# A fused linear-attention and GEGLU kernel: the head halves of batch 0 loaded in the order of use, and its first units in another order

## Chip, cores and metric

One core of one Trainium2 chip. The metric is the device time of one execution in microseconds (us); a quoted time is the median of several executions, in brackets lowest and highest. All executions that are compared were fast, with a granted TensorE clock of 0.99 to 1.00. Ratios are the mean time of one kernel's fast runs over that of the other's in the same rounds, so not quite the ratio of the medians.

## The reference

```python
q_p = concat(relu(q) * cos, relu(q) * sin)      # by position, batch 8, heads 8, seq 576, dim 64
k_p = concat(relu(k) * cos, relu(k) * sin)
kv  = k_p^T v ;  z = sum_s k_p                  # per head, 128 x 64 and 128
x   = (q_p kv) / (q_p z + 1e-6)                 # heads side by side: 4608 x 512
out = (gelu(x @ w_gate) * (x @ w_val)) @ w_out  # 512 -> 1536 -> 512
```

## The kernel before

Everything is scheduled by hand; each engine runs its instructions in the order of the program. A *front* brings batch 0 to its first 128 columns of transposed x. *Units* follow: a gate (four matmuls, then Gelu on ACT) and a value (four matmuls, then a product on VectorE), for one of twelve slices `jt` of 128 hidden channels and some columns of x (`*A` is columns 0 to 255, `*Bw` 256 to 575). While the first units run, the remaining tiles of batch 0 are still normalized and transposed between them. "Dummies" are matmuls on junk, meant to keep the TensorE clock up. An *evacuation* copies a result of TensorE out of the tile `ps`, whose last-but-one index is called a bank; a *hole* is time in which TensorE has nothing to do between two groups of matmuls. `sk` and `sq` scale k and q by cosine or sine, a *numerator* is q_p kv, a *norm* the division by q_p z. "Guards" are copies of one element into a weight tile: the weight loads, issued by GpSimd, must wait for them.

```python
load(kf, k, 0, 0, 4, nc.scalar)      # heads 0-3; the other half of its rows on the SP queue
load(kf, k, 0, 4, 8)
# ... memsets, iota
load(qf, q, 0, j1=2)                 # tiles 0 and 1 of q
load(vf, v, 0, 0, 4)
load(vf, v, 0, 4, 8)
load(qf, q, 0, j0=2)
# ... tables, identity
dummies(26)
for h0 in (0, 4):
    for j in range(NJ + 1):
        sk(j, 0, "v", h0, h0 + 4)                        # k scale with cosine: VectorE
        sk(j, 1, "v" if j < 2 else "s", h0, h0 + 4)      # with sine: VectorE or ACT
nc.scalar.copy(wg_sb[0:2, 0, 0:1], qf[0:2, 7, 1, D - 1:D])   # guard: weights after q has landed
load_w(0, 2); load_w(2, 4); load_w(4, 8)
for j in range(2):
    sq(j, 0, "v"), sq(j, 1, "s")
    q_by_pe(0, j, j, None)                               # transposes
dummies(3)
q_evac(0, 0, 0, "v")
cast_v(0, 0, 2, "v"); cast_v(0, 2, 4, "s")
kv_half(0, 0, 4, None)                                   # k^T v of heads 0-3
q_evac(0, 1, 1, "v")
dummies(2)
cast_v(0, 4, 6, "v"); cast_v(0, 6, 8, "s")
kv_evac(0, 0, 4, "v")
kv_half(0, 1, 5, "s")                                    # heads 4-7
# ... numerators of tiles 0 and 1, norms on VectorE, transposes of x tile 0, of q tile 2
gate(0, 0, 0, 128, 5); gate(0, 1, 0, 128, 4)
# ... units, with X(t) = transposes of x tile t and Y(t) = its numerators and norm between them
```

Of the kernel before, what the change touches and what calls it, by code (L numbers as in the profile page):

```python
# [10 lines left out]
BF16 = mybir.dt.bfloat16  # L11
# [5 lines left out]
def kernel(  # L17
# [10 lines left out]
    nc = tc.nc  # L28

    B, H, S, D = q.shape  # L30
# [4 lines left out]
    CT = C // 128  # L35
# [40 lines left out]
    def load(dst, t, b, h0=0, h1=H, even=None, odd=None, j0=0, j1=NJ + 1):  # L76
        runs = t[b, h0:h1].rearrange("h (i r) d -> i h r d", r=9)
        for s, r0, n, eng in ((1, 5, 4, odd), (0, 0, 5, even)):
            n = min(n, j1)
            (eng or nc.sync).dma_start(  # L80
                out=dst[s:128:2, h0:h1, j0:n].rearrange("p h j d -> p h (j d)"),
                in_=runs[:, :, r0 + j0:r0 + n].rearrange("i h r d -> i h (r d)"),
            )
# [4 lines left out]
    pos_i = sb.tile([128, NJ + 1], mybir.dt.int32, name="pos_i")  # L88
    par_i = sb.tile([128, 1], mybir.dt.int32, name="par_i")
    load(kf, k, 0, 0, 4, nc.scalar)  # L90
    load(kf, k, 0, 4, 8)
    nc.vector.memset(junk, 0.0)
    nc.gpsimd.iota(par_i, pattern=[[1, 1]], base=0, channel_multiplier=1)
    nc.gpsimd.iota(pos_i, pattern=[[2, NJ + 1]], base=0, channel_multiplier=9)
    half_pi = sb.tile([128, 1], FP32, name="half_pi")
    nc.gpsimd.memset(half_pi, math.pi / 2.0)
    nc.gpsimd.memset(qf[:, :, NJ], 0.0)  # L97
    nc.gpsimd.memset(vf[:, :, NJ], 0.0)  # L98
    load(qf, q, 0, j1=2)
    load(vf, v, 0, 0, 4)  # L100
    load(vf, v, 0, 4, 8)
    load(qf, q, 0, j0=2)

# [21 lines left out]
    def dummies(n, bank=7):  # L125
        for _ in range(n):
            nc.tensor.matmul(ps[:, bank, :], lhsT=junk[:, 0:128], rhs=junk, start=True, stop=True)  # L127
# [11 lines left out]
    def cast_v(b, h0, h1, eng="v"):  # L139
        cp = nc.vector.tensor_copy if eng == "v" else nc.scalar.copy  # L140
        cp(vx[b % 2][:, :, h0:h1, 0:D], vf[:, h0:h1].rearrange("p h j d -> p j h d"))  # L141
# [9 lines left out]
    def kv_half(b, g, bank, eng="s"):  # L151
        for h in range(4 * g, 4 * g + 4):
            for j in range(NJ + 1):
                nc.tensor.matmul(  # L154
                    ps[:, bank, (h % 4) * (D + 1):(h % 4 + 1) * (D + 1)],
                    lhsT=kp[:, j, h, :],
                    rhs=vx[b % 2][:, j, h, 0:D + 1],
                    start=(j == 0), stop=(j == NJ),
                )
        if eng is not None:  # L160
            kv_evac(b, g, bank, eng)

    def kv_evac(b, g, bank, eng):
        src = ps[:, bank, 0:4 * (D + 1)].rearrange("p (h e) -> p h e", e=D + 1)
        dst = kv[b % 2][:, 4 * g:4 * g + 4, 0:D + 1]
        (nc.scalar.copy if eng == "s" else nc.vector.tensor_copy)(dst, src)

    def numer_mm(b, t, bank, g, rows=128):
        for h in range(4 * g, 4 * g + 4):
            nc.tensor.matmul(  # L170
                ps[0:rows, bank + g, (h % 4) * (D + 1):(h % 4 + 1) * (D + 1)],
                lhsT=qT[b % 2][:, t, h, 0:rows],
                rhs=kv[b % 2][:, h, 0:D + 1],
                start=True, stop=True,
            )

    def norm(xb, bank, g0, g1, rows=128):

        n = g1 - g0
        nd = ps[0:rows, bank + g0:bank + g1, 0:4 * (D + 1)].rearrange("p g (h e) -> p g h e", e=D + 1)  # L180
        den = rot.tile([128, 2, 4], FP32, name="den")
        nc.vector.tensor_scalar(den[0:rows, 0:n], nd[:, :, :, D], EPS, None, op0=ALU.add)  # L182
        rec = rot.tile([128, 2, 4], FP32, name="rec")
        nc.vector.reciprocal(rec[0:rows, 0:n], den[0:rows, 0:n])
        nc.vector.tensor_tensor(  # L185
            xb[0:rows, g0:g1], nd[:, :, :, 0:D],
            rec[0:rows, 0:n, :, None].to_broadcast([rows, n, 4, D]), op=ALU.mult,
        )

    def new_xb():  # L190
        return rot.tile([128, 2, 4, D], BF16, name="xb", bufs=4)
# [30 lines left out]
        gels[n, jt, c0] = gel = rot.tile([128, 512], FP32, name="gel", bufs=4)  # L222
        nc.scalar.activation(gel[:, 0:w], ps[:, gb, 0:w], AF.Gelu)  # L223

    def value(n, jt, c0, w, vb):

        p0 = starts[n] + c0
        for ct in range(CT):
            nc.tensor.matmul(  # L229
                ps[:, vb, 0:w], lhsT=wv_sb[:, ct, jt * 128:(jt + 1) * 128],  # L230
                rhs=xT[:, ct, p0:p0 + w], start=(ct == 0), stop=(ct == CT - 1),
            )
        gel = gels.pop((n, jt, c0))
        nc.vector.tensor_mul(hT[n % 2][:, jt, 64 + c0:64 + c0 + w], gel[:, 0:w], ps[:, vb, 0:w])  # L234

# [68 lines left out]
    def load_w(j0, j1):  # L304
        nc.gpsimd.dma_start(out=wg_sb[:, :, j0 * 128:j1 * 128], in_=wg_r[:, :, j0 * 128:j1 * 128])
        nc.gpsimd.dma_start(out=wv_sb[:, :, j0 * 128:j1 * 128], in_=wv_r[:, :, j0 * 128:j1 * 128])
# [13 lines left out]
    def q_by_pe(b, j, bank, eng, h0=0, h1=H):  # L320

        qb = ps[:, bank, :].bitcast(BF16).rearrange("p (h t) -> p h t", h=H)
        for h in range(h0, h1):
            nc.tensor.transpose(out=qb[:, h, :], in_=qp[:, j, h, :], identity=ident)  # L324
        if eng is not None:
            q_evac(b, j, bank, eng, h0, h1)

    def q_evac(b, j, bank, eng, h0=0, h1=H):
        qb = ps[:, bank, :].bitcast(BF16).rearrange("p (h t) -> p h t", h=H)
        cp = nc.vector.tensor_copy if eng == "v" else nc.scalar.copy  # L330
        if j < NJ:
            cp(qT[b % 2][:, j, h0:h1], qb[:, h0:h1])
        else:
            cp(qT[b % 2][:, j, h0:h1, 0:64], qb[:, h0:h1, 0:128:2])

    def x_by_pe(b, t, xb, bank, eng, c0=0, c1=CT):
        p0 = b * S + t * 128
        cp = nc.vector.tensor_copy if eng == "v" else nc.scalar.copy
        xb2 = xb.rearrange("p g h d -> p (g h d)")
        rows = 128 if t < NJ else 64  # L340
        view = ps[:, bank, 0:256].bitcast(BF16).rearrange("p (c t) -> p c t", c=CT)
        for ct in range(c0, c1):
            nc.tensor.transpose(  # L343
                out=view[:, ct, 0:rows], in_=xb2[0:rows, ct * 128:(ct + 1) * 128], identity=ident[0:rows, 0:rows],
            )
        cp(xT[:, c0:c1, p0:p0 + rows], view[:, c0:c1, 0:rows])  # L346

    def sq(j, which, eng, *h):
        scale(Q, j, which, eng, *h)

    def sk(j, which, eng, *h):
        scale(K, j, which, eng, *h)


    dummies(26)
    for h0 in (0, 4):
        for j in range(NJ + 1):
            sk(j, 0, "v", h0, h0 + 4)
            sk(j, 1, "v" if j < 2 else "s", h0, h0 + 4)
    nc.scalar.copy(wg_sb[0:2, 0, 0:1], qf[0:2, 7, 1, D - 1:D])  # L360
    load_w(0, 2)
    load_w(2, 4)
    load_w(4, 8)
    for j in range(2):
        sq(j, 0, "v"), sq(j, 1, "s")
        q_by_pe(0, j, j, None)
    dummies(3)
    q_evac(0, 0, 0, "v")
    cast_v(0, 0, 2, "v")
    cast_v(0, 2, 4, "s")  # L370
    kv_half(0, 0, 4, None)
    q_evac(0, 1, 1, "v")
    dummies(2)
    cast_v(0, 4, 6, "v")
    cast_v(0, 6, 8, "s")
    kv_evac(0, 0, 4, "v")
    kv_half(0, 1, 5, "s")
    x0, x1 = new_xb(), new_xb()
    numer_mm(0, 0, 6, 0)
    norm(x0, 6, 0, 1)  # L380
    dummies(1, 4)
    numer_mm(0, 0, 6, 1)
    sq(2, 1, "s")
    norm(x0, 6, 1, 2)
    sq(2, 0, "v")
    numer_mm(0, 1, 0, 0)
    numer_mm(0, 1, 0, 1)
    norm(x1, 0, 0, 2)
    x_by_pe(0, 0, x0, 4, "s", 0, 2)
    dummies(2, 5)  # L390
    x_by_pe(0, 0, x0, 4, "s", 2, 4)
    q_by_pe(0, 2, 3, None)

    nc.gpsimd.tensor_copy(tiny[0:1, 1:2], x0[0:1, 1, 3, D - 1:D])
    load_w(8, 12)
# [5 lines left out]
    def X(t, bank, eng):  # L401
        return lambda: x_by_pe(0, t, xs[t], bank, eng)
# [4 lines left out]
        return f  # L407

    gate(0, 0, 0, 128, 5)
    gate(0, 1, 0, 128, 4)  # L410
    X(1, 2, "s")()
    q_evac(0, 2, 3, "v")
    sq(3, 0, "v"), sq(3, 1, "s")
    value(0, 0, 0, 128, 6)
    value(0, 1, 0, 128, 7)
    Y(2, 0)()
    gate(0, 0, 128, 128, 5)
    gate(0, 1, 128, 128, 4)
    value(0, 0, 128, 128, 2)
    value(0, 1, 128, 128, 3)  # L420
    q_by_pe(0, 3, 6, "s")
    gate(0, 2, *A, 5)
    X(2, 0, "v")()
    sq(4, 1, "s"), sq(4, 0, "v")
    gate(0, 3, *A, 4)
    value(0, 2, *A, 7)
    Y(3, 0)()
    value(0, 3, *A, 2)
    q_by_pe(0, 4, 3, "s")
    gv_unit(0, 0, 256, 128, 5, 6)  # L430
    gv_unit(0, 1, 256, 128, 4, 7, (X(3, 0, "s"),))
    Y(4, 2)()
    gv_unit(0, 0, 384, 128, 5, 1)
    gv_unit(0, 1, 384, 128, 4, 0)
    gate(0, 4, *A, 5)
    X(4, 7, "v")()
    gate(0, 5, *A, 4)
    gv_unit(0, 2, *Bw, 2, 6)
    gv_unit(0, 3, *Bw, 3, 7)
    value(0, 4, *A, 1)  # L440
    value(0, 5, *A, 2)
    gv_unit(0, 0, 512, 64, 4, 6)
    gv_unit(0, 1, 512, 64, 5, 7)


    load_q(1, nc.gpsimd)
# [164 lines left out]
```

## Time and profile before

| | before |
|---|---|
| time, median of 6 (range) | 325.78 us (325.57 to 326.11) |
| span of the profiled execution | 324.3 us |
| TensorE busy, with dummies | 315.1 us |
| first gate matmul | 16.88 us |
| end of block 0's first units (first gate of jt 4, columns 256 to 575) | 29.88 us |
| last matmul ends / rest of the span | 319.63 us / 4.67 us |

### The profile page before, as it was taken

The page shows a single profiled execution, that of the slowest core. Times are in us where ns is not written, and L with a number is a line of the kernel's source. Part 1 is how long each engine was busy: PE and PEld are TensorE (multiplying, and loading weights), DVE is VectorE, ACT ScalarE, POOL GpSimd, SP SyncE. Part 2 cuts the span into 40 slices and gives each one's busy share as a digit, 9 for nine tenths or more (in the row PEclk, how much of TensorE's full clock was granted, in tenths as well). Part 3 has the DMA queues.
Part 4 walks back from the last instruction along what each step waited for, and adds up shares of the span by engine and source line. Part 5 has one row for each costly group of instructions (what it writes and reads, how often), then busy time and mean ns, then how long its engine had stood idle before and what let it go on. Part 6 is the DMA issues. An engine that isn't in the chain of part 4 may idle for free.

```text
span 324.3 us, 5829 instructions
## 1 busy us (share of the span) xinstructions
PE 315.1 (97%) x2185; PEld 167.1 (52%) x2218; DVE 168.0 (52%) x380; ACT 151.3 (47%) x271; POOL 21.7 (7%) x43
## 2 busy tenths in 40 slices
PE   7899999999999999999999999999999999999994
PEld 3587866455445544544455445544554444444443
DVE  4885776677564576366636574647454222222210
ACT  5674764853583248325642565237522222323321
POOL 2551000001100010001000100010000100100000
PEclk9999999999999999999999999999999999999999
DMA  7999999999899939991999289936333111000124
GB/s 223 287 204 275 226 307 306 324 200 172 282 222 345 219 51 194 333 236 51 195 324 242 50 153 294 301 68 124 104 73 75 32 32 34 32 32 32 37 63 98
DMA packets 88300, 55.56 MB, mean 171 GB/s; under 512 B 53072, under 2 KB 83536, under 8 KB 88272
## 3 DMA queue, kind: packets, MB, share of 16 engines
q1 hardware_dynamic: 81744, 48.84, 60.8%
q0 software_dynamic: 6096, 5.90, 10.2%
q10 hardware_dynamic: 432, 0.46, 0.4%
q8 instruction: 17, 0.28, 0.3%
q14 instruction: 11, 0.09, 0.1%
HBM read 37.75 MB, written 9.44 MB: 146 GB/s over the span
## 4 chain that ended last, share of the span: by engine, by line
PE 93%; DMA 2%; SPq 1%; DVE 1%; issue 1%; POOL 0%; ACT 0%; POOLq 0%; DVEq 0%
PE ps L218 29%; PE ps L229 29%; PE ps L259 28%; PE ps L170 3%; PE ps L154 3%; DMA vf<-in_v_dram 2%; SPq L80 1%; PE ps L277 1%; PE ps L324 1%; PE ps L343 1%; DVE vx L141 0%; ACT xT L346 0%; DVE qp L135 0%; POOL vf L98 0%; POOL qf L97 0%
## 5 line engine op out<-in xcount | busy, mean ns | idle before, releaser
L234 DVE TENSOR_TENSOR hT<-gel,ps 128x512 bf16<-128x512 f32 (+5 forms) x126 | 76.1, 607 | 89.3 <-PE ps L229 88.4
L218 PE MATMUL ps<-xT,wg_sb 128*128 128x512 bf16 (+5 forms) x492 | 111.8, 348 | 0.7
L229 PE MATMUL ps<-xT,wv_sb 128*128 128x512 bf16 (+5 forms) x496 | 111.8, 348 | 0.4
L223 ACT ACTIVATE gel<-ps 128x512 f32<-128x512 f32 (+5 forms) x126 | 67.4, 536 | 74.2 <-PE ps L218 51.9
L259 PE MATMUL ps<-wo_sb,hT 128*128 128x512 bf16 x408 | 94.3, 379 | 0.6
L218 PEld LDWEIGHTS <-wg_sb 128*128 128x128 bf16 x504 | 47.1, 98 | 44.5
L229 PEld LDWEIGHTS <-wv_sb 128*128 128x128 bf16 x504 | 45.7, 98 | 39.0
L259 PEld LDWEIGHTS <-hT 128*128 128x128 bf16 x420 | 40.8, 98 | 47.7
L288 ACT COPY o_sb<-ps 128x512 f32<-128x512 f32 x35 | 20.5, 586 | 76.2 <-PE ps L259 69.9
L185 DVE TENSOR_TENSOR xb<-ps,rec 128x512 bf16<-128x512 f32 (+2 forms) x41 | 27.8, 678 | 2.8 <-DMA xr<-xb 1.4
L182 DVE TENSOR_SCALAR den<-ps 128x8 f32<-128x8 f32 (+2 forms) x41 | 6.7, 163 | 42.2 <-PE ps L170 42.2
L137 ACT ACTIVATE kp<-kf,sin_c 128x512 bf16<-128x512 f32 (+1 forms) x41 | 25.4, 681 | 0.8 <-DMA kf<-in_k_dram 0.8
L170 PEld LDWEIGHTS <-qT 128*128 128x128 bf16 (+1 forms) x320 | 15.1, 98 | 8.3 <-issue 0.4
L137 ACT ACTIVATE qp<-qf,sin_c 128x512 bf16<-128x512 f32 x28 | 19.3, 713 | 0.1
L135 DVE TENSOR_SCALAR kp<-kf,cos_c 128x512 bf16<-128x512 f32 (+1 forms) x45 | 18.1, 450 | 1.4 <-DMA kf<-in_k_dram 1.4
L135 DVE TENSOR_SCALAR qp<-qf,cos_c 128x512 bf16<-128x512 f32 x40 | 18.2, 495 | 0.0
L209 POOL COPY xT<-xr 128x256 bf16<-128x256 bf16 x7 | 2.8, 402 | 208.7 <-DMA xr<-xb 208.7
L170 PE MATMUL ps<-kv,qT 128*128 128x65 bf16 (+1 forms) x320 | 16.6, 194 | 0.1
L154 PEld LDWEIGHTS <-kp 128*128 128x128 bf16 x320 | 10.9, 97 | 2.6 <-issue 0.7
L127 PE MATMUL ps<-hT 128*128 128x512 bf16 x33 | 10.2, 460 | 1.8 <-DVE par_i L104 1.7
L154 PE MATMUL ps<-vx,kp 128*128 128x65 bf16 x320 | 11.2, 193 | 0.1
L141 ACT CAST vx<-vf 128x1280 bf16<-128x1280 f32 (+1 forms) x9 | 9.7, 1076 | 1.2 <-DMA vf<-in_v_dram 1.2
(54 smaller groups left out, 88.6 us busy)
## 6 DMA issues: line engine op xcount, KB each, us to landing
out_dram<-o_sb SPq DMA_DIRECT2D x38, 128.0 KB, 2.4
kf<-in_k_dram SPq DMA_DIRECT2D x7, 640.0 KB, 7.3
out_dram<-o_sb SPq DMA_DIRECT2D x16, 256.0 KB, 2.9
qf<-in_q_dram SPq DMA_DIRECT2D x6, 640.0 KB, 6.2
vf<-in_v_dram SPq DMA_DIRECT2D x6, 640.0 KB, 8.7
kf<-in_k_dram SPq DMA_DIRECT2D x7, 512.0 KB, 6.2
qf<-in_q_dram SPq DMA_DIRECT2D x6, 512.0 KB, 4.9
vf<-in_v_dram SPq DMA_DIRECT2D x6, 512.0 KB, 7.8
```

Source lines behind the costliest of these rows:

```text
L127: nc.tensor.matmul(ps[:, bank, :], lhsT=junk[:, 0:128], rhs=junk, start=True, stop=True)
L135: nc.vector.tensor_scalar(d, s, col, 0.0, op0=ALU.mult, op1=ALU.max)
L137: nc.scalar.activation(d, s, AF.Relu, scale=col)
L154: nc.tensor.matmul(ps[:, bank, (h % 4) * (D + 1):(h % 4 + 1) * (D + 1)], lhsT=kp[:, j, h, :], rhs=vx[b % 2][:, j, h, 0:D + 1], start=(j == ...
L170: nc.tensor.matmul(ps[0:rows, bank + g, (h % 4) * (D + 1):(h % 4 + 1) * (D + 1)], lhsT=qT[b % 2][:, t, h, 0:rows], rhs=kv[b % 2][:, h, 0:D ...
L185: nc.vector.tensor_tensor(xb[0:rows, g0:g1], nd[:, :, :, 0:D], rec[0:rows, 0:n, :, None].to_broadcast([rows, n, 4, D]), op=ALU.mult,)
L218: nc.tensor.matmul(ps[:, gb, 0:w], lhsT=wg_sb[:, ct, jt * 128:(jt + 1) * 128], rhs=xT[:, ct, p0:p0 + w], start=(ct == 0), stop=(ct == CT - 1),
L223: nc.scalar.activation(gel[:, 0:w], ps[:, gb, 0:w], AF.Gelu)
L229: nc.tensor.matmul(ps[:, vb, 0:w], lhsT=wv_sb[:, ct, jt * 128:(jt + 1) * 128], rhs=xT[:, ct, p0:p0 + w], start=(ct == 0), stop=(ct == CT - 1),
L234: nc.vector.tensor_mul(hT[n % 2][:, jt, 64 + c0:64 + c0 + w], gel[:, 0:w], ps[:, vb, 0:w])
L259: nc.tensor.matmul(ps[:, bank, :], lhsT=hT[n % 2][:, jt, c0:c0 + 128], rhs=wo_sb[:, jt, :], start=(jt == 0), stop=(jt == JT - 1),)
L288: nc.scalar.copy(o_sb, ps[:, bank, :])
```

## The change

The intent: v of heads 0 to 3 is needed before k of heads 4 to 7, so load in the order in which the halves are consumed, start the first k-v half 2 us earlier, and do what belongs to heads 0 to 3 of tiles 0 and 1 while the other half is still on its way. The first units are rearranged around it. The core of the diff:

```diff
     load(kf, k, 0, 0, 4, nc.scalar)
-    load(kf, k, 0, 4, 8)
...
     load(qf, q, 0, j1=2)
     load(vf, v, 0, 0, 4)
+    load(kf, k, 0, 4, 8)
     load(vf, v, 0, 4, 8)
...
-    dummies(26)
-    for h0 in (0, 4): ...k scales of both halves, then the guard on q and the weight loads
+    dummies(19)
+    ...k scales of heads 0-3 only
     for j in range(2):
         sq(j, 0, "v"), sq(j, 1, "s")
         q_by_pe(0, j, j, None)
     dummies(3)
     q_evac(0, 0, 0, "v")
+    q_evac(0, 1, 1, "s", 0, 4)
+    nc.scalar.copy(wg_sb[0:2, 0, 0:1], vf[0:2, 3, 3, D - 1:D])      # guard now on v of heads 0-3
+    load_w(0, 2); load_w(2, 4); load_w(4, 8)
     cast_v(0, 0, 2, "v"); cast_v(0, 2, 4, "s")
+    q_evac(0, 1, 1, "v", 4, 8)
+    kv_half(0, 0, 4, "s")
+    dummies(2)
+    numer_mm(0, 0, 6, 0); numer_mm(0, 1, 0, 0)      # heads 0-3 of tiles 0 and 1
+    for j in range(NJ + 1):
+        sk(j, 0, "v", 4, 8)                         # k scales of heads 4-7: now here
+        sk(j, 1, "v" if j < 1 else "s", 4, 8)
+    norm(x0, 6, 0, 1)
     cast_v(0, 4, 6, "v"); cast_v(0, 6, 8, "s")
+    dummies(8)
+    x_by_pe(0, 0, x0, 4, "s", 0, 2)
     kv_half(0, 1, 5, "s")
+    norm(x1, 0, 0, 1)
+    ...second halves of the numerators, norms and transposes, x tile 1 in two parts
 # units
-    gate(0, 2, *A, 5); X(2, 0, "v")(); sq(4, ...); gate(0, 3, *A, 4); value(0, 2, *A, 7); Y(3, 0)(); ...
+    gate(0, 2, *A, 7); X(2, 2, "v")(); product(...) x2; gate(0, 3, *A, 6); q_by_pe(0, 3, 1, "s")
+    gate(0, 0, 256, 128, 3); gate(0, 1, 256, 128, 5); sq(4, ...); value(0, 2); value(0, 3); Y(3, 6)()
+    value(0, 0, 256); value(0, 1, 256); q_by_pe(0, 4, 3, "s"); gate(0, 4, *A, 0); X(3, 6, "s")(); ...
```

More of the change, by code (lines that the diff above doesn't have):

```diff
@@ L96 @@
     nc.gpsimd.memset(half_pi, math.pi / 2.0)
+    nc.gpsimd.memset(vf[:, :, NJ], 0.0)
     nc.gpsimd.memset(qf[:, :, NJ], 0.0)
-    nc.gpsimd.memset(vf[:, :, NJ], 0.0)
     load(qf, q, 0, j1=2)
     load(vf, v, 0, 0, 4)
+    load(kf, k, 0, 4, 8)
     load(vf, v, 0, 4, 8)
@@ L223, in gate, with value @@
         nc.scalar.activation(gel[:, 0:w], ps[:, gb, 0:w], AF.Gelu)
-    def value(n, jt, c0, w, vb):
+    def value(n, jt, c0, w, vb, now=True):
         p0 = starts[n] + c0
@@ L232, in value, with product @@
             )
+        if now:
+            product(n, jt, c0, w, vb)
+    def product(n, jt, c0, w, vb):
         gel = gels.pop((n, jt, c0))
@@ L336, in x_by_pe @@
     def x_by_pe(b, t, xb, bank, eng, c0=0, c1=CT):
-        p0 = b * S + t * 128
-        cp = nc.vector.tensor_copy if eng == "v" else nc.scalar.copy
         xb2 = xb.rearrange("p g h d -> p (g h d)")
@@ L345, in x_by_pe, with x_evac @@
             )
+        if eng is not None:
+            x_evac(b, t, bank, eng, c0, c1)
+    def x_evac(b, t, bank, eng, c0=0, c1=CT):
+        p0 = b * S + t * 128
+        cp = nc.vector.tensor_copy if eng == "v" else nc.scalar.copy
+        rows = 128 if t < NJ else 64
+        view = ps[:, bank, 0:256].bitcast(BF16).rearrange("p (c t) -> p c t", c=CT)
         cp(xT[:, c0:c1, p0:p0 + rows], view[:, c0:c1, 0:rows])
@@ L352, in sk @@
         scale(K, j, which, eng, *h)
-    dummies(26)
-    for h0 in (0, 4):
-        for j in range(NJ + 1):
-            sk(j, 0, "v", h0, h0 + 4)
-            sk(j, 1, "v" if j < 2 else "s", h0, h0 + 4)
-    nc.scalar.copy(wg_sb[0:2, 0, 0:1], qf[0:2, 7, 1, D - 1:D])
-    load_w(0, 2)
-    load_w(2, 4)
-    load_w(4, 8)
+    dummies(19)
+    for j in range(NJ + 1):
+        sk(j, 0, "v", 0, 4)
+        sk(j, 1, "v" if j < 2 else "s", 0, 4)
     for j in range(2):
@@ L368 @@
     q_evac(0, 0, 0, "v")
+    q_evac(0, 1, 1, "s", 0, 4)
+    nc.scalar.copy(wg_sb[0:2, 0, 0:1], vf[0:2, 3, 3, D - 1:D])
+    load_w(0, 2)
+    load_w(2, 4)
+    load_w(4, 8)
     cast_v(0, 0, 2, "v")
     cast_v(0, 2, 4, "s")
-    kv_half(0, 0, 4, None)
-    q_evac(0, 1, 1, "v")
+    q_evac(0, 1, 1, "v", 4, 8)
+    kv_half(0, 0, 4, "s")
     dummies(2)
+    x0, x1 = new_xb(), new_xb()
+    numer_mm(0, 0, 6, 0)
+    numer_mm(0, 1, 0, 0)
+    for j in range(NJ + 1):
+        sk(j, 0, "v", 4, 8)
+        sk(j, 1, "v" if j < 1 else "s", 4, 8)
+    norm(x0, 6, 0, 1)
     cast_v(0, 4, 6, "v")
     cast_v(0, 6, 8, "s")
-    kv_evac(0, 0, 4, "v")
+    dummies(8)
+    x_by_pe(0, 0, x0, 4, "s", 0, 2)
     kv_half(0, 1, 5, "s")
-    x0, x1 = new_xb(), new_xb()
-    numer_mm(0, 0, 6, 0)
-    norm(x0, 6, 0, 1)
-    dummies(1, 4)
+    norm(x1, 0, 0, 1)
+    sq(2, 0, "v"), sq(2, 1, "s")
+    dummies(1, 3)
+    x_by_pe(0, 1, x1, 2, None, 0, 2)
     numer_mm(0, 0, 6, 1)
-    sq(2, 1, "s")
     norm(x0, 6, 1, 2)
-    sq(2, 0, "v")
-    numer_mm(0, 1, 0, 0)
     numer_mm(0, 1, 0, 1)
-    norm(x1, 0, 0, 2)
-    x_by_pe(0, 0, x0, 4, "s", 0, 2)
-    dummies(2, 5)
+    norm(x1, 0, 1, 2)
+    dummies(1, 3)
     x_by_pe(0, 0, x0, 4, "s", 2, 4)
+    x_evac(0, 1, 2, "s", 0, 2)
     q_by_pe(0, 2, 3, None)
+    q_evac(0, 2, 3, "s", 0, 4)
     nc.gpsimd.tensor_copy(tiny[0:1, 1:2], x0[0:1, 1, 3, D - 1:D])
@@ L409 @@
     gate(0, 0, 0, 128, 5)
+    x_by_pe(0, 1, x1, 2, "v", 2, 4)
+    q_evac(0, 2, 3, "v", 4, 8)
     gate(0, 1, 0, 128, 4)
-    X(1, 2, "s")()
-    q_evac(0, 2, 3, "v")
-    sq(3, 0, "v"), sq(3, 1, "s")
-    value(0, 0, 0, 128, 6)
-    value(0, 1, 0, 128, 7)
-    Y(2, 0)()
-    gate(0, 0, 128, 128, 5)
-    gate(0, 1, 128, 128, 4)
-    value(0, 0, 128, 128, 2)
-    value(0, 1, 128, 128, 3)
-    q_by_pe(0, 3, 6, "s")
-    gate(0, 2, *A, 5)
-    X(2, 0, "v")()
-    sq(4, 1, "s"), sq(4, 0, "v")
-    gate(0, 3, *A, 4)
-    value(0, 2, *A, 7)
-    Y(3, 0)()
-    value(0, 3, *A, 2)
-    q_by_pe(0, 4, 3, "s")
-    gv_unit(0, 0, 256, 128, 5, 6)
-    gv_unit(0, 1, 256, 128, 4, 7, (X(3, 0, "s"),))
-    Y(4, 2)()
-    gv_unit(0, 0, 384, 128, 5, 1)
-    gv_unit(0, 1, 384, 128, 4, 0)
-    gate(0, 4, *A, 5)
-    X(4, 7, "v")()
-    gate(0, 5, *A, 4)
-    gv_unit(0, 2, *Bw, 2, 6)
+    sq(3, 0, "v")
+    gate(0, 0, 128, 128, 6)
+    gate(0, 1, 128, 128, 7)
+    sq(3, 1, "s")
+    value(0, 0, 0, 128, 0)
+    value(0, 1, 0, 128, 1)
+    Y(2, 2)()
+    value(0, 0, 128, 128, 5, False)
+    value(0, 1, 128, 128, 4, False)
+    gate(0, 2, *A, 7)
+    X(2, 2, "v")()
+    product(0, 0, 128, 128, 5)
+    product(0, 1, 128, 128, 4)
+    gate(0, 3, *A, 6)
+    q_by_pe(0, 3, 1, "s")
+    gate(0, 0, 256, 128, 3)
+    gate(0, 1, 256, 128, 5)
+    sq(4, 1, "s"), sq(4, 0, "v")
+    value(0, 2, *A, 0)
+    value(0, 3, *A, 4)
+    Y(3, 6)()
+    value(0, 0, 256, 128, 1)
+    value(0, 1, 256, 128, 2)
+    q_by_pe(0, 4, 3, "s")
+    gate(0, 4, *A, 0)
+    X(3, 6, "s")()
+    gate(0, 5, *A, 4)
+    gate(0, 0, 384, 128, 5)
+    Y(4, 1)()
+    value(0, 0, 384, 128, 7)
+    gv_unit(0, 1, 384, 128, 3, 6)
+    value(0, 4, *A, 4)
+    X(4, 1, "v")()
+    value(0, 5, *A, 0)
+    gv_unit(0, 2, *Bw, 2, 5)
     gv_unit(0, 3, *Bw, 3, 7)
-    value(0, 4, *A, 1)
-    value(0, 5, *A, 2)
-    gv_unit(0, 0, 512, 64, 4, 6)
-    gv_unit(0, 1, 512, 64, 5, 7)
+    gv_unit(0, 0, 512, 64, 1, 6)
+    gv_unit(0, 1, 512, 64, 2, 4)
     load_q(1, nc.gpsimd)
```

## The prediction

> **What bounds the kernel now.** I read the page first: busy shares, then the slices.
>
> ```profile
> PE 315.1 (97%) x2185; PEld 167.1 (52%) x2218; DVE 168.0 (52%) x380; ACT 151.3 (47%) x271; POOL 21.7 (7%) x43
> ...
> PE   7899999999999999999999999999999999999994
> ...
> PEclk9999999999999999999999999999999999999999
> ```
>
> TensorE is the bound: 315.1 of 324.3 us, at full clock, and only the first two slices (16 us) and the last are not full. Part of "full" there is fill: the row "L127 PE MATMUL ps<-hT" holds 33 dummies that compute nothing. The change touches only the first 30 us and adds no work, so the question is when the stream of real matmuls starts and how many holes it has until block 0's first units are done. After that nothing but TensorE ends a wait, so a shift there goes to the end one for one.
>
> The chain of waits, cut to 6 to 30 us (start, us, what):
>
> ```profile
> 6.25 6.45 DMA vf<-in_v_dram
> ...
> 12.80 0.64 DVE vx L141
> ...
> 13.48 0.76 PE ps L154 x20
> 14.24 0.14 PE ps L170 x4
> ...
> 14.81 0.42 DVE xb L185
> ...
> 15.89 0.49 DVE qp L135
> ...
> 16.42 0.62 PE ps L324 x8
> 17.04 0.45 PE ps L218 x8
> ...
> 23.64 0.59 ACT xT L346
> ```
>
> The front hangs on the landing of v of heads 4 to 7 at 12.70, the last but one of the loads that the front needs; from there 4.2 us of casts, k-v products, numerators and transposes lead to the first gate matmul. The timeline of TensorE gives that moment and the holes after it (start, us of the group, line):
>
> ```profile
> 16.42 0.62 PE L324 MATMUL ps<-ident,qp 128*128 128x128 bf16 x8
> 16.88 0.61 PE L218 MATMUL ps<-xT,wg_sb 128*128 128x128 bf16 x8
> 17.46 0.40 PE L343 MATMUL ps<-ident,xb 128*128 128x128 bf16 x4
> ...
> 18.14 0.42 PE L170 MATMUL ps<-kv,qT 128*128 128x65 bf16 x8
> 18.53 0.61 PE L218 MATMUL ps<-xT,wg_sb 128*128 128x128 bf16 x8
> ...
> 23.43 0.39 PE L229 MATMUL ps<-xT,wv_sb 128*128 128x128 bf16 x4
> 23.75 0.44 PE L170 MATMUL ps<-kv,qT 128*64 128x65 bf16 x8
> 24.27 0.38 PE L218 MATMUL ps<-xT,wg_sb 128*128 128x128 bf16 x4
> ```
>
> Groups overlap in their drain, so I use starts. Eight gate matmuls of 128 columns should take 0.45 (the next eight do) but last 0.58: a hole of 0.13. Eight numerators take 0.25, last 0.39: 0.14. Around tile 4: 0.10 and 0.27. One more of 0.10 at 25.6. The first gate starts at 16.88 and the holes until block 0's first units end at 29.88 sum to 0.74.
>
> **What the Trainium skill says.** "DMA: Bandwidth & Descriptors", section "Anatomy of one DMA — SWDGE (gpsimd) path": about 2.0 us of a transfer is fixed, mostly the receipt after the last byte. The trace agrees in kind: the bytes ahead of the end of q tiles 0 and 1 (1.70 MB) had moved by about 7.8, it landed at 9.4, a lag of 1.6. Its Specifications give a first byte of about 1 us to a GpSimd issue; here the first weight packet moves about 3.0 us after the issue at 9.92, and the measurement decides. "TensorE: Matmul & The Clock Gate", Part 1, says that the array runs at half rate until about 3.4 us of sustained work; the dummies start every 0.43 until about 6.3 and every 0.21 after, so it agrees in kind. "ScalarE: Activation LUTs", "What ACT_TABLE_LOAD costs": back-to-back ACTIVATEs overlap by about 93 ns; two of 0.72 take 1.33 here, an overlap of 0.11.
>
> **The loads.** Landings now: k 0-3 5.1, k 4-7 7.7, q tiles 0-1 9.4, v 0-3 11.05, v 4-7 12.7, q tiles 2-4 14.7. The engines move 0.33 to 0.36 MB per us without a break, so a new order permutes landings and does not shorten the sum: q at about 7.5, v 0-3 at 9.4, k 4-7 at 11.05, v 4-7 again at 12.7. That is the heart of my forecast: the landing that the front hangs on doesn't move. What can be gained lies behind it, and there the change puts more in DVE's way.
>
> **The front, step by step** (durations from the rows of before, 0.05 from one engine's end to another's start).
> - Dummies: 11 x 0.43 and 8 x 0.21 from 1.75 end at 8.25. q sine and cosine 7.5 to 8.85; transposes at 8.28 and 8.90 (before 10.29).
> - DVE evacuates tile 0 8.95-9.6, casts v 0-1 9.56-10.1. ACT evacuates half of tile 1 9.55-10.15, guard copy to 10.3, casts v 2-3 10.2-10.9. First k-v half 10.2-11.4 (before 12.16-12.92). ACT evacuates it by 11.85; eight numerators at 11.9 (before 14.07).
> - DVE: six k scales at a pitch of 0.265 from the landing 11.07, to 12.66; norm of x0's first half (0.16, 0.19, 0.42) to 13.48; only then the cast of v 4-5, 13.40-13.95. Before, that cast ran 12.80-13.43. ACT: four k scales at 0.43, 11.95-13.7, cast of v 6-7 to 14.4.
> - Second k-v half 14.0-14.87 (before 13.48-14.24), evacuated at 15.3 (before 14.66). So the half that came last is 0.6 later.
> - Numerators 15.34; norm of x0's second half 15.67-16.5 (before 15.15-15.97); its transposes 16.55 (before 16.04); evacuation 16.86-17.23. Eight q transposes follow and the first gate starts at about 17.13 (before 16.88; there 0.28 was lost to a q scale that is now done early).
>
> So the gate starts 0.25 later, with two x transposes more behind it (0.11).
>
> **The units.** Work is the same. Holes, each from a latency against the TensorE work put beside it:
> - third matmul of gate 0 waits for the x evacuation: 0.06; x1's other transposes wait for ACT in their bank (17.54): 0.15; gate of tile 1 waits for DVE's evacuation at 18.2: 0.22.
> - Tile 2: numerators at 19.0, norm 1.1 plus 0.4 to start it; two values and a gate (0.88) beside it: 0.45.
> - q tile 4: ACT does tile 3's evacuation (1.01), two gelus, then the q sine (0.72), about 2.85 from the transposes of tile 3 on; beside it 2.47 of matmuls: 0.38.
> - x tile 3: ACT has qT of tile 4 (0.59) and a gelu (0.38) ahead of the evacuation (0.59), and one gate of 0.44 lies beside it: 0.50 (before 0.27).
> - x tile 4: 0.25 and 0.10.
>
> Sum 2.11, against 0.74: +1.37. With the start: 0.25 - 0.11 + 1.37 = **+1.5 us**. I take two thirds, +1.0: the new counts of dummies fit this timeline so well (19 end at 8.25, the transposes can start at 8.28) that the order was evidently tuned on something like it, and such plain holes as 0.4 and 0.5 may be smaller than I make them. 325.8 + 1.0 = **326.8 us**.
>
> **Rivals.**
> - The front wins: v 0-3 is there 1.65 earlier and the numerators of both tiles' first halves are out of the way. If the cast of v 4-7 isn't held by DVE (k landing at 10.7 rather than 11.05, or v 4-7 at 12.3), the gate starts at 16.5, and with holes near the old 0.74 the time is 325.3. Against it: DVE has 2.4 us of work between k's landing and that cast.
> - Weights become the wait. The guard copy ends at 10.3, not 9.6, so the weights are issued 0.6 later: gate 0-1 land at 16.4 (now 9.92 + 5.9 = 15.8), value 0-1 17.7, gate 2-3 19.0, value 2-3 20.5. My timeline needs them at 17.1, 18.6, 19.7 and 22.2, so they just fit. A front that wins would run into them at gate 2, which caps its gain at about 0.5. If they slip over 1 us, the time is about 327.6.
> - The other loads of block 0 and batch 1 come later with the units and TensorE waits around 37 or 45. Output weights are waited for only by GpSimd (9.6 us), so there is slack, and it changes nothing.
>
> **Range and chances.** 2% is 6.5 us; the whole front lasts 16.9 us and the landing at 12.7 leaves 4.2 of it, and all holes after it are 0.74, so no step here can move the time by that much. Same is nearly sure. Repeats differ by 0.5 us. 325.4 to 327.9 covers from a small gain to the full sum and a weights slip. Faster by over 2%: 0.01; within: 0.985; slower: 0.005.
>
> **What would show it.** Right: landings of q, v, k, v at about 7.5, 9.4, 11.05, 12.7; the first k-v half near 10.2; the DVE cast of v 4-5 near 13.4, behind k scales and a norm; the first gate near 17.1; holes ahead of x tile 2, q tile 4 and behind x tile 3; equal gaps from 32 us on. Wrong: a first gate before 16.8, or holes below 1 us, which would make the change a small gain; or a weight transfer as what ends a wait of TensorE.

## The result, and the profile after

| | before | changed |
|---|---|---|
| time, median of 6 (range) | 325.78 us (325.57 to 326.11) | 328.64 us (328.17 to 328.71) |
| ratio, 95% interval | | 1.0085 (1.0072 to 1.0098) |
| first k-v half / second k-v half starts | 12.16 / 13.48 us | 10.19 / 14.38 us |
| first gate matmul | 16.88 us | 17.39 us |
| first units end | 29.88 us | 31.98 us |
| last matmul ends / rest of the span | 319.63 / 4.67 us | 321.74 / 5.16 us |

The change is 2.86 us slower, far outside of the noise and outside of the range of the prediction, though under 1%. Matching the matmuls of the two traces one to one, the shift is 2.10 us at the end of the first units and 2.10 at each landmark from there to the last matmul: nothing is given back or lost in the 290 us between. Another 0.5 comes after the last matmul.

The timeline of TensorE of the changed kernel (start, us of the group, engine, line, operation; in brackets the idle time before it and what ended it):

```profile
8.32 1.23 PE L328 MATMUL ps<-ident,qp 128*128 128x128 bf16 x16
...
10.19 0.46 PE L154 MATMUL ps<-vx,kp 128*128 128x65 bf16 x10
...
14.38 0.76 PE L154 MATMUL ps<-vx,kp 128*128 128x65 bf16 x20 [0.18 <-DVE den L182]
...
16.82 0.28 PE L345 MATMUL ps<-ident,xb 128*128 128x128 bf16 x2 [0.58 <-DVE xb L185]
...
17.39 0.45 PE L218 MATMUL ps<-xT,wg_sb 128*128 128x128 bf16 x4
...
20.04 0.60 PE L218 MATMUL ps<-xT,wg_sb 128*128 128x256 bf16 x4
20.99 0.40 PE L345 MATMUL ps<-ident,xb 128*128 128x128 bf16 x4 [0.35 <-DVE xb L185]
...
25.45 0.60 PE L218 MATMUL ps<-xT,wg_sb 128*128 128x256 bf16 x4
26.39 0.38 PE L218 MATMUL ps<-xT,wg_sb 128*128 128x128 bf16 x4 [0.34 <-ACT xT L356]
```

The q transposes (8.32) and the first k-v half (10.19) are where the prediction put them, 2 us earlier than before. The second k-v half is at 14.38, 0.9 later than before. Two of the holes forecast can be read from the starts: a gate of 256 columns takes 0.44, so from 20.04 to 20.99 there is a hole of 0.51 ahead of x tile 2, and from 25.45 to 26.39 one of 0.50 behind x tile 3. (The brackets are shorter, as they count from a group's modelled end.) In the same way: 0.23 and 0.28 around x tile 1, 0.20 at q tile 4, and 0.22 twice and 0.26 around tile 4. Their sum is 2.42, against the 0.74 of before.

The chain of waits of the changed kernel, at the place where before it read "DMA vf" (start, us, what):

```profile
4.93 5.82 DMA kf<-in_k_dram
...
10.84 2.28 DVE kp L135 x6
...
13.77 0.55 DVE vx L141
...
14.39 0.76 PE ps L154 x20
```

The front no longer hangs on the landing of v of heads 4 to 7 but on that of k of heads 4 to 7 (10.74) and on what VectorE does after it. Six k scales take 2.28 us here (2.20 from the first start to the start of what follows them); I had reckoned with 1.6, by starts.

### The profile page after: what moved, and what is told of

Same layout as the page of the kernel before. It is cut to its first block, busy times and chain, and to the rows that moved or that the text cites. A ratio compares the mean times of both kernels' runs of the same rounds, so it can differ in the third digit from the quotient of the medians.

```text
span 326.9 us, 5866 instructions
## 1 busy us (share of the span) xinstructions
PE 317.7 (97%) x2218; PEld 166.8 (51%) x2218; DVE 168.1 (51%) x382; ACT 152.2 (47%) x275; POOL 21.7 (7%) x43
## 4 chain that ended last, share of the span: by engine, by line
PE 92%; DVE 2%; DMA 2%; SPq 1%; issue 1%; ACT 1%; DVEq 0%; ACTq 0%
PE ps L218 28%; PE ps L229 28%; PE ps L263 28%; PE ps L170 3%; PE ps L154 3%; DMA kf<-in_k_dram 2%; SPq L80 1%; PE ps L281 1%; PE ps L328 1%; DVE kp L135 1%; PE ps L345 1%; DVE hT L238 0%; DVE xb L185 0%; ACT gel L223 0%; DVE rec L184 0%
## 5 line engine op out<-in xcount | busy, mean ns | idle before, releaser
L218 PE MATMUL ps<-xT,wg_sb 128*128 128x512 bf16 (+5 forms) x504 | 113.6, 348 | 0.5 <-ACT xT L356 0.3
L229 PE MATMUL ps<-xT,wv_sb 128*128 128x512 bf16 (+5 forms) x504 | 113.0, 348 | 0.0
L263 PE MATMUL ps<-wo_sb,hT 128*128 128x512 bf16 x420 | 96.5, 379 | 0.0
L127 PE MATMUL ps<-hT 128*128 128x512 bf16 x34 | 10.5, 456 | 1.7 <-DVE par_i L104 1.7
```

Source lines behind the costliest of these rows:

```text
L127: nc.tensor.matmul(ps[:, bank, :], lhsT=junk[:, 0:128], rhs=junk, start=True, stop=True)
L218: nc.tensor.matmul(ps[:, gb, 0:w], lhsT=wg_sb[:, ct, jt * 128:(jt + 1) * 128], rhs=xT[:, ct, p0:p0 + w], start=(ct == 0), stop=(ct == CT - 1),
L229: nc.tensor.matmul(ps[:, vb, 0:w], lhsT=wv_sb[:, ct, jt * 128:(jt + 1) * 128], rhs=xT[:, ct, p0:p0 + w], start=(ct == 0), stop=(ct == CT - 1),
L263: nc.tensor.matmul(ps[:, bank, :], lhsT=hT[n % 2][:, jt, c0:c0 + 128], rhs=wo_sb[:, jt, :], start=(jt == 0), stop=(jt == JT - 1),)
```

## The experiments

All with correct results. "Gate" is the first gate matmul, "units" the end of the first units, "tail" the time from the last matmul's end to the end of the span, all from the profiled execution; ratios are to the kernel before, of the same rounds.

| run | median us | ratio | gate | units | tail | VectorE records |
|---|---|---|---|---|---|---|
| before | 325.78 | | 16.88 | 29.88 | 4.67 | 577 |
| changed | 328.64 | 1.0085 | 17.39 | 31.98 | 5.16 | 578 |
| e1 new front, old units | 326.90 | 1.0033 | 17.17 | 30.08 | 5.26 | 578 |
| e2 old front, new units | 327.63 | 1.0051 | 16.42 | 31.62 | 4.43 | 575 |
| e3 cast first | 327.97 | 1.0065 | 16.70 | 31.28 | 4.87 | 578 |
| e4 old load order | 329.79 | 1.0116 | 18.48 | 33.07 | 5.07 | 578 |
| e5 before, ACT +5 | 325.85 | 0.9999 | 16.57 | 29.56 | 4.64 | 577 |
| e6 changed, ACT +6 | 328.60 | 1.0079 | 17.46 | 32.06 | 5.28 | 578 |
| e7 two holes filled | 327.51 | 1.0048 | 17.38 | 31.50 | 4.44 | 579 |
| e8 before, early guard | 327.62 | 1.0064 | 18.80 | 33.18 | 4.66 | 577 |
| e9 before, VectorE +1 | 326.17 | 1.0008 | 16.59 | 29.58 | 4.86 | 578 |
| e10 changed, VectorE +1 | 328.05 | 1.0060 | 17.59 | 32.18 | 4.46 | 579 |
| e11 e3's front, old units | 325.79 | 0.9999 | 16.88 | 29.79 | 4.45 | 579 |
| e12 before, gate 4 earlier | 325.73 | 0.9996 | 16.75 | 29.63 | 4.71 | 577 |
| e13 changed, late guard | 330.89 (one) | | 18.23 | 34.60 | 4.64 | 577 |
| e14 e11 and e12 | 325.90 | 0.9996 | 17.07 | 29.87 | 4.48 | 579 |

The last column counts all of VectorE's records in the trace, semaphore waits included. The gate jitters from trace to trace with the landings; the length of the units doesn't (13.00, 12.99, 12.99 in before, e5 and e9; 14.59 or 14.60 in changed, e6 and e10).

### e1 and e2: which half of the change costs what

Theory: two separate losses, one in the front and one in the units. Rival: the holes of the units are an echo of a late front.

e1 takes the changed kernel's loads and front and puts back the old units (and the whole-tile evacuations that they need); e2 is the other way round.

```diff
 # e1, on the changed kernel
-    x_by_pe(0, 1, x1, 2, None, 0, 2)
-    x_evac(0, 1, 2, "s", 0, 2)
-    q_evac(0, 2, 3, "s", 0, 4)
-    ...the new units
+    ...the units of before
 # e2, on the changed kernel
-    ...the new loads and front
+    ...the loads and front of before
     gate(0, 0, 0, 128, 5)
-    x_by_pe(0, 1, x1, 2, "v", 2, 4)
+    x_by_pe(0, 1, x1, 2, None); x_evac(0, 1, 2, "s", 0, 2); x_evac(0, 1, 2, "v", 2, 4)
+    q_evac(0, 2, 3, "s", 0, 4)
```

> New loads and front, old unit order. Two parts theory (front +0.4, units +1.7, about 0.6 after the last matmul): first gate at 17.4 as in the changed kernel, the units take 13.0 us as before, so the matmul stream is 0.5 later than before and the time 0.5 to 1.1 above before. Rival, that the holes of the units are only an echo of the late front: they stay with the old order too, stream 1.5 to 2.1 later, time 2 to 2.8 above before.

> Old loads and front, new unit order. Two parts theory: first gate at 16.9, holes of the units near 2.2 instead of 0.74, stream 1.4 to 1.8 later than before, time 1.5 to 2.4 above before. Rival (echo of the front): holes near 0.8, time within 0.4 of before.

Measured: e1 1.0033 (1.0020 to 1.0047), e2 1.0051 (1.0039 to 1.0064). In us of the 325.8, that is about 1.1 and 1.7, together 2.7 of the 2.8 of the whole change: the two losses are separate and, within the noise, add up. In e1 the units take 12.91 from the gate on; in e2 they take 15.20 although the gate is at 16.42. The echo falls. e2's units are 0.61 longer than the changed kernel's because all transposes of x tile 1 stand behind the gate there: the holes around that tile sum to 0.98 against 0.51, and two transposes more take 0.11.

e1's matmul stream ends only 0.21 later than in the profile of before, and yet it is 1.1 slower. Half of that is the tail, 5.26 instead of 4.67; the profile of before is also a late sample of its own front: its execution was the slowest of the six (326.12 us), and its gate is later than those of e2, e5, e9 and e12, which have that front and start at 16.42, 16.57, 16.59 and 16.75. The five gates of the old front have a mean of 16.64, and the five with the changed front and nothing else in it (17.39, e1 17.17, e6 17.46, e7 17.38, e10 17.59) one of 17.40. The front costs 0.76 at the gate, not the 0.51 of the first pair of traces.

### e3: VectorE's queue in the front

```diff
-    norm(x0, 6, 0, 1)
     cast_v(0, 4, 6, "v")
     cast_v(0, 6, 8, "s")
-    dummies(8)
-    x_by_pe(0, 0, x0, 4, "s", 0, 2)
+    norm(x0, 6, 0, 1)
+    dummies(6)
     kv_half(0, 1, 5, "s")
     norm(x1, 0, 0, 1)
     sq(2, 0, "v"), sq(2, 1, "s")
-    dummies(1, 3)
+    x_by_pe(0, 0, x0, 4, "s", 0, 2)
```

> Changed kernel with VectorE's cast of v 4-5 ahead of the norm of x0's first half (and that half's transposes behind the second k-v half). If VectorE's queue holds the second k-v half: it starts at 13.6 instead of 14.4, the first gate at about 16.9 instead of 17.4, time 0.3 to 0.5 below the changed kernel. Rival, that the landing or ACT's cast holds it: second half past 14.1, gate past 17.2, no gain.

VectorE's cast and the second k-v half in e3's timeline:

```profile
12.71 0.54 DVE L141 CAST vx<-vf 128x640 bf16<-128x640 f32 x1
...
13.31 0.89 PE L154 MATMUL ps<-vx,kp 128*128 128x65 bf16 x20
```

The second k-v half starts at 13.31, 1.07 earlier than in the changed kernel. Of that, 0.33 is k's earlier start in this trace (first scale at 10.51 instead of 10.84); the rest is VectorE's order, as the cast comes 2.20 us after the first scale instead of 2.93. The gate is at 16.70, 0.7 below the mean of the changed front; e11 and e14 below, which have the same order (and two transposes fewer ahead of the gate), start at 16.88 and 17.07, so about 0.5 is the better estimate, from the three. The ratio falls from 1.0085 to 1.0065, some 0.65 us, though the two intervals (1.0072 to 1.0098 and 1.0051 to 1.0079) overlap a little. What held the second half was VectorE's order, the norm in front of the cast, and not the landing.

### e4: the load order alone

```diff
     load(kf, k, 0, 0, 4, nc.scalar)
+    load(kf, k, 0, 4, 8)
 ...
-    load(kf, k, 0, 4, 8)
     load(vf, v, 0, 4, 8)
```

The order of the two memsets goes back with it.

> Changed kernel with only the load order of before. Landings back to k 4-7 at 7.7, q 9.4, v 0-3 11.05. If the order of loads gains what it was made for (first numerators 2 us earlier) and this reaches the end: over 0.5 slower than the changed kernel. If the landing of v 4-7 and VectorE's work behind it set the front anyway: VectorE gets the k scales after the first cast all the same (about 12.6), the first gate comes 0.3 to 1.0 later, and holes stay the same.

Gate at 18.48, 1.1 later, and 1.0116. So within the new front the new load order is worth 1.0 us and does what it was made for; the arrangement needs it and then spends more than that elsewhere. The guard moved with v, so the weights are issued later too (11.91 instead of 10.56), but the first lands at 16.35, well before the gate. My second guess in the expectation, 0.3 to 1.0, was at its end.

### e5, e6, e9, e10: what lengthens the tail

All stores at the end are the same, but the tail differed: 5.16 against 4.67, and 5.26 in e1. In the traces with a long tail a packet of 8 KB of the instruction queue moves about 1 us before the last store's data end; in those with a short one it comes 2 us after them. My first theory was that ACT's number of instructions sets its moment, since the kernels with a long tail had 237 or 238 rows on ACT and the others 233 or 234.

```diff
 # e5 (5 places) and e6 (6 places): into block 0's units of jt 4 to 11
+    for i, u in enumerate([(4, 1), (5, 1), (6, 0), (6, 1), (10, 0), (11, 0)]):
+        between[u] = between.get(u, ()) + (L(nc.scalar.copy, tiny[0:1, 2 + i:3 + i], half_pi[0:1]),)
```

> Kernel before plus five ACT copies of one element, placed where ACT idles (jt 4 to 11 of block 0); 238 rows on ACT as in the changed kernel instead of 233. In the traces so far the kernels with 237 or 238 ACT rows have an instruction fetch of 8 KB about 1.1 us before the last store's data ends, and 4.9 to 5.3 us from the last matmul to the end; those with 233 or 234 have the fetch after the data and 4.4 to 4.7. If the fetch's moment follows ACT's count and delays the stores: matmul stream within 0.2 of before, end of span 0.4 to 0.6 later, time 0.4 to 0.6 above before. If the longer tail is chance: time within 0.2 of before.

> Changed kernel plus six such copies (244 rows on ACT). If the fetch's moment follows ACT's count, it now lies well before the last stores: tail back to 4.4 to 4.7, time 0.4 to 0.6 below the changed kernel (ratio to before near 1.007 instead of 1.0085). If the tail is chance or set by the front itself: no change.

Both missed: 0.9999 and 1.0079, tails 4.64 and 5.28 as without the copies, the fetch where it was. The ACT theory fell. e7, made for another reason (below), gave the hint: it moves one operation from ACT to VectorE, and there the fetch came 11 us before the end and the tail was 4.44. Counted by VectorE, all ten traces fell into place, so I added one instruction to VectorE:

```diff
 # e9 on the kernel before, e10 on the changed one
         (10, 1): (L(load_q, 2), ),
+        (6, 0): (L(nc.vector.memset, tiny[0:1, 7:8], 0.0), ),
```

> Kernel before plus one memset of one element on VectorE. Counting VectorE's records in the traces: 575 or 577 in the four kernels whose last instruction fetch comes 2 us after the stores (tail from the last matmul to the end 4.4 to 4.7), 578 in the five with the fetch 1 us before the stores end (tail 4.9 to 5.3), 579 in the one with it 11 us before (tail 4.4). If VectorE's count sets the fetch and the fetch the tail: 578 records here, fetch about 1 us before the end of the stores, tail 4.9 to 5.3, matmul stream unchanged, time 0.4 to 0.8 above before (ratio 1.0012 to 1.0025). If the count is a coincidence: time within 0.2 of before.

> Changed kernel plus the same memset: 579 records on VectorE. If the count sets it: fetch about 11 us before the end, tail 4.4 to 4.7, matmul stream as in the changed kernel (units end near 32.0), time 0.4 to 0.8 below the changed kernel, ratio to before 1.006 to 1.0073. If not: 1.0085 again.

Both fetches moved as forecast: with 578 records it comes 0.98 us before the last store's data end, with 579 11.1 us before. The DMA queues in the last 3.7 us with stores (packets, MB, share of 16 engines). The kernel before, 318.9 to 322.6:

```profile
q1 hardware_dynamic: 313, 0.38, 45.8%
q10 hardware_dynamic: 160, 0.13, 14.8%
```

e9, 318.6 to 322.3:

```profile
q1 hardware_dynamic: 314, 0.38, 45.4%
q10 hardware_dynamic: 160, 0.13, 15.2%
q14 instruction: 1, 0.01, 1.0%
```

The same stores, and in e9 one instruction packet among them. Over all sixteen traces the six with 578 records have tails of 4.86 to 5.28, mean 5.08; the ten others 4.43 to 4.71, mean 4.56. In time: e10 is at 1.0060, where the changed kernel and e6 were at 1.0085 and 1.0079, some 0.6 to 0.8 us less, though its units ended 0.1 to 0.2 later than theirs. e9 is 0.27 us slower than before, below what I expected, and its interval (0.9996 to 1.0021) holds 1. So the count sets the moment of the fetch, and a fetch in the middle of the stores goes with a tail that is 0.5 longer; the exact price in time stays between 0.3 and 0.8. The packets of the stores show where the tail comes from. In the ten traces without a fetch there, the last store's data end 2.53 to 2.55 us after the last matmul; in the six with it, 2.78 to 3.17, and in those only five to nine of some 385 packets end after 2.57, one behind the other; the rest end as everywhere. So the fetch goes with a few packets held back by 0.23 to 0.62 us. How long follows when the fetch ends (2.23 us after the last matmul in e3, 2.50 in e1), not its length (0.44 and 0.32). That these packets share its DMA engine fits this but is not shown, as the trace kept here doesn't name the engine of a packet.

### e7: the holes of the units

```diff
     gate(0, 2, *A, 7)
-    X(2, 2, "v")()
-    product(0, 0, 128, 128, 5)
-    product(0, 1, 128, 128, 4)
     gate(0, 3, *A, 6)
+    X(2, 2, "v")()
+    product(0, 0, 128, 128, 5)
+    product(0, 1, 128, 128, 4)
...
-    X(3, 6, "s")()
+    X(3, 6, "v")()
```

> Changed kernel with x tile 2's transposes behind gate 3 instead of gate 2, and x tile 3 evacuated by VectorE instead of ACT. If the holes are what I say (norm latency ahead of x tile 2, ACT's queue ahead of x tile 3's evacuation): 0.51 falls to 0.1 or less, 0.50 to about 0.2, the stream ends 0.6 to 0.8 earlier, time 0.5 to 0.9 below the changed kernel. If weights or banks hold those places: no change.

The timeline of TensorE of e7, at the two places:

```profile
20.03 1.04 PE L218 MATMUL ps<-xT,wg_sb 128*128 128x256 bf16 x8
20.98 0.40 PE L345 MATMUL ps<-ident,xb 128*128 128x128 bf16 x4
...
25.00 0.40 PE L345 MATMUL ps<-ident,xb 128*128 128x128 bf16 x4
25.24 1.06 PE L218 MATMUL ps<-xT,wg_sb 128*128 128x256 bf16 x8
26.23 0.44 PE L170 MATMUL ps<-kv,qT 128*64 128x65 bf16 x8
```

Two gates of 0.44 now lie before x tile 2, and the hole of 0.51 is down to 0.07. From x tile 3's evacuation on, 25.24 to 26.23 holds 0.66 of matmuls and 0.33 of holes, where the changed kernel had 0.60 (its 0.50 and 0.10 ahead of tile 4's numerators). The hole of 0.20 at q tile 4 is gone too. But 0.23 came back ahead of the gate of tile 2's columns and 0.20 ahead of x tile 3. Net, the units take 14.12 instead of 14.59: 0.47 gained, less than the 0.6 to 0.8 expected. The causes were right, the sizes too large: a hole that is filled uncovers part of the next latency. The time fell by 1.2 us, to 1.0048, because its VectorE count happens to be 579: about 0.5 from the stream and the rest with the tail.

### e8 and e13: GpSimd's issues and VectorE's scales

The six k scales of heads 4 to 7 in the changed kernel take 2.28 us; they run while GpSimd issues the weight loads (10.56 to 15.24). Theory: the issues slow them. Rival: writes of the transfers do. e8 puts the issues beside the same scales in the kernel before; e13 takes them away in the changed one.

```diff
 # e8, on the kernel before
     for h0 in (0, 4):
         ...k scales
+        if h0 == 0:
+            nc.scalar.copy(wg_sb[0:2, 0, 0:1], kf[0:2, 3, 1, D - 1:D])
-    nc.scalar.copy(wg_sb[0:2, 0, 0:1], qf[0:2, 7, 1, D - 1:D])
 # e13, on the changed kernel
-    nc.scalar.copy(wg_sb[0:2, 0, 0:1], vf[0:2, 3, 3, D - 1:D])
-    load_w(0, 2); load_w(2, 4); load_w(4, 8)
 ...behind the k scales of heads 4-7
+    nc.scalar.copy(wg_sb[0:2, 0, 0:1], kf[0:2, 7, 3, D - 1:D])
+    load_w(0, 2); load_w(2, 4); load_w(4, 8)
```

> Kernel before with the weights' guard on k of heads 0 to 3, so that GpSimd issues from about 7.2 us, beside VectorE's k scales of heads 4 to 7 (7.7 to 9.7). If GpSimd's issuing slows VectorE's f32 SBUF scales: their pitch goes from 0.265 to about 0.4 there, up to 0.6 for one. Otherwise it stays 0.265. First weight packets: near 10.2 if the 3 us from issue are the making of descriptors, near 12.9 if the other loads come first. The time: within 0.6 of before either way, slower if weights take bandwidth from v.

> Changed kernel with the weights' guard behind ACT's k scales of heads 4 to 7, so that GpSimd issues nothing before about 13 us. If GpSimd's issuing is what slows those scales on VectorE: six of them take 1.6 instead of 2.28 us, none over 0.36, and the cast of v 4-5 starts about 2.2 us after the first of them instead of 2.93; it is then at most held by the landing of v 4-7. If the slow scales come from something else (DMA writes): 2.2 to 2.3 us again. The gate waits for weights (first at about 19), so the time is worse by 1 to 2.5 and is not the point.

The next four fences are the same view of VectorE's scales, by shape, from about 7.2 or 10.5 us on (duration in ns min/median/max, first and last start in us). The kernel before:

```profile
L135 DVE TENSOR_SCALAR kp<-kf,sin_c x2: 346/346/346, 8.0 to 8.5; 128x256 bf16<-128x256 f32 x2
```

e8, the same scales beside issues:

```profile
L135 DVE TENSOR_SCALAR kp<-kf,sin_c x2: 532/565/598, 7.7 to 8.4; 128x256 bf16<-128x256 f32 x2
L135 DVE TENSOR_SCALAR qp<-qf,cos_c x2: 695/757/819, 9.9 to 10.6; 128x512 bf16<-128x512 f32 x2
```

The changed kernel:

```profile
L135 DVE TENSOR_SCALAR kp<-kf,cos_c x5: 333/352/598, 10.8 to 12.6; 128x256 bf16<-128x256 f32 x5
```

e13, its scales with no issue beside them:

```profile
L135 DVE TENSOR_SCALAR kp<-kf,cos_c x5: 349/349/353, 11.1 to 12.4; 128x256 bf16<-128x256 f32 x5
```

Beside issues single scales take up to 598 ns, and the q scales of 478 take 695 and 819; without issues all take 345 to 353. Among these scales the slow one is in both traces each time the one that ends just after the next issue has begun (issues begin at 11.50, 12.23 and 12.96 in the changed kernel, at 8.15, 8.88, 9.61, 10.34 and 11.07 in e8); scales that begin and end within one issue are not slowed. In e13 the six k scales take 1.67 and the cast of v 4-5 starts 2.33 us after the first of them (11.09 to 13.41), 2.93 in the changed kernel (10.84 to 13.77). Theory shown, in both directions, and the rival falls: the loads were being written at the same rate beside e13's scales (317 GB/s from 11.1 to 12.8) as beside the changed kernel's (309 from 10.8 to 13.1). e13 is one execution, but its six scales lie within 5 ns of each other. Its time tells nothing, as the gate waits 0.93 for weights.

e8 also shows the other end of the guard's place: with weights issued at 7.27, their first packet moves at 11.37 us, neither near 10.2 nor at 12.9, and they then share the DMA engines with q. The kernel is 2.1 us slower by the mean, 1.7 by the medians (more than I expected). v is not what pays for it: its last half lands at 12.42, no later than before (12.71). q of tiles 2 to 4 does, at 17.13 instead of 14.63, and VectorE's scale of q tile 2, which stands ahead of the first gate, waits for it:

```profile
17.22 0.49 DVE L135 TENSOR_SCALAR qp<-qf,cos_c 128x512 bf16<-128x512 f32 x1 [1.02 <-DMA qf<-in_q_dram]
```

Its profiled execution was its slowest (329.42), so its gate of 18.80 is not typical.

### e11, e12 and e14: a version that beats both?

e11 is e3's front with the old units and one more memset on VectorE; e12 is the kernel before with one gate pulled ahead; e14 is both.

```diff
 # e12
     Y(4, 2)()
-    gv_unit(0, 0, 384, 128, 5, 1)
-    gv_unit(0, 1, 384, 128, 4, 0)
     gate(0, 4, *A, 5)
+    gv_unit(0, 0, 384, 128, 4, 1)
+    gv_unit(0, 1, 384, 128, 6, 0)
     X(4, 7, "v")()
     gate(0, 5, *A, 4)
+    value(0, 4, *A, 1)
...
-    value(0, 4, *A, 1)
```

> New loads and front with the cast of v 4-5 first, old unit order, one memset more on VectorE. If the three parts are separate and add up (front with VectorE's queue mended: gate at 16.7; units 13.0; tail 4.5): stream end within 0.3 of before, time within 0.4 of before, no better. If the new load order has a gain hidden by the queue: 0.5 or more below before.

> Kernel before with gate 4 of columns 0 to 255 moved ahead of the two units that wait for x tile 3's evacuation, to fill the hole of 0.27 there. If holes of the unit stretch are worth their full length at the end: stream 0.2 to 0.3 earlier, time 0.2 to 0.3 below before. If not, or if weights 4 to 7 (landing 22.4) now hold it: no gain or a loss.

> New loads and front with the cast first, old unit order with gate 4 pulled ahead, 579 records on VectorE. If the parts add up: 0.1 to 0.3 below before, ratio 0.999 to 1.000; it would be the fastest version, though hardly beyond noise. If the new front has no gain left: within 0.1 of before.

e11 0.9999 (0.9986 to 1.0011): with VectorE's order mended, the old units and the fetch out of the way, the whole loss is gone, and no gain shows behind it. e12 0.9996: the hole of 0.27 shrank to 0.13 and the units are 0.12 shorter, less than expected. e14 0.9996 (0.9982 to 1.0009): its units are 12.80 long, the shortest of all, its gate at 17.07. Neither beats the kernel before by more than noise.

## Why the prediction was wrong

The direction and the places were right; the size was not: +1.0 forecast, +2.86 measured, outside of the range. By its own steps:

- **Loads: right in time, wrong in role.** q scales start at 7.55 (forecast 7.5), the first k-v half at 10.19 (10.2), k of heads 4 to 7 landed at 10.74 (11.05), and v of heads 4 to 7 in time for a cast that came late for other reasons. But what I called the heart of my forecast, that the front goes on hanging on the landing of v of heads 4 to 7, failed: the chain now runs through k of heads 4 to 7 and VectorE, as my own steps had it. (The page that I cited for the lag is about issues by GpSimd, and these loads are issued by SP and ACT: the agreement is one of size only.) The first rival's condition even came true (k at 10.74, its 10.7), and the gate was still 0.9 later than the 16.5 it gave. e4 shows that the new order is worth 1.0 us within the new front.
- **"the gate starts 0.25 later": mis-sized.** It is 0.76 by five traces of each front. Of the missing 0.51, 0.24 is the reference: I took 16.88 from one trace, and the old front's mean is 16.64 (that trace was of the slowest of six executions). The other 0.27 is in the changed front (17.40, forecast 17.13), and its term is "six k scales at a pitch of 0.265": they took 2.20 us by starts instead of 1.6, as they now run beside GpSimd's issues; k's landing 0.31 before my forecast made up half of that, by luck. e13 restores 1.58 (first start to last end 1.67, against 2.28) by moving the issues. The Trainium skill, "SBUF — State Buffer", section "Who interferes with whom", says that VectorE in a two-port mode contends with GpSimd and that `tensor_scalar` can enter one. I hadn't looked that page up; traces agree in kind (2.28 us with issues beside the scales, 1.67 without).
- **"Sum 2.11, against 0.74": nearly right, low.** Measured 2.42. The largest forecast holes are there: 0.45 ahead of x tile 2 (0.51), 0.50 behind x tile 3 (0.50); at q tile 4 0.20 instead of 0.38; around tile 4 0.70 instead of 0.35. The units are 1.59 longer, where hole and work terms gave 1.26 (1.37 less 0.11).
- **"I take two thirds": wrong.** I read the fit of the dummies as a sign that the order had been tuned until plain holes were gone. The traces had the holes. The step took 0.5 off a sum that was already low.
- **Missing: the tail.** I wrote that after block 0 a shift goes to the end one for one, which holds for the matmuls to 0.01 us, but a change that adds one VectorE instruction also moves an instruction fetch. It now falls among the last stores, with a tail longer by 0.5 in the traces.

With measured sizes the terms are: front 0.76, units 1.59, tail about 0.5, sum 2.85, against 2.86; that it agrees so closely is luck, as the front's and the tail's terms are known to 0.2 at best. Of the rivals, the weights' later issue was no wait: the gate weights land at 15.55, 18.42 and 23.12, and the gates that use them start at 17.39, 20.04 and 25.45. What stays open is the exact price of the fetch, and whether it acts through a DMA engine that it shares with stores.

## What to carry to other kernels

When a load order is changed so that something can start sooner, follow the engine that must serve both halves: here VectorE got the k scales, a norm and a cast into one queue ahead of the last half, beside GpSimd's issues, and the early start was spent there. Holes worked out from latency against the work put beside it were worth their full length at the end; don't discount them because the code looks tuned. For differences under 1 us take the reference point from several traces, and look at the tail after the last matmul too, since one instruction more can shift a fetch into the last stores.

## What the Trainium skill lacked or had wrong

- "SBUF — State Buffer", "Who interferes with whom", has the contention of VectorE with GpSimd, and that the loser blocks for the whole of the other's instruction. By the issues' records of 0.76 to 0.95 us it is milder here: a scale of 0.35 took at most 0.60 and one of 0.48 took 0.70 to 0.82. Of these scales only the one running as the next issue began was slowed; those within one issue took 0.33 to 0.35.
- "DMA: Bandwidth & Descriptors", Specifications, gives about 1 us to the first byte of a GpSimd issue. No first weight load here was so quick: its first packet came 1.60 us after the first issue at the least (e4, e13), 2.84 in the kernel before (the prediction's "about 3.0"), 4.1 in e8. The longer waits are not the issue's own latency alone: in thirteen kernels that issue first between 9.31 and 10.79, the first packet moves between 12.65 and 12.93, whenever it was issued. What it waits for was not tested.
- "Runtime: NRT & Kernel Launch", "Instruction fetch mechanics", has that the sequencer fetches instructions through a DMA queue of its own, and calls the cost mostly hidden. It lacks that such a fetch can fall among the last stores, where it shows: here packets of 8 KB, 0.31 to 0.66 us, moved there by one VectorE instruction (578 records against 577 or 579), with tails of 5.08 in the mean against 4.56 without.
